# Retention and a mixture of experts on one core: a branch placed ahead of the last three scatters, the last product in two column halves, and five earlier places in the queues

## The chip, the core and the metric

The kernel runs on one core of a Trainium2 chip. The core has a matrix engine (TensorE, PE in the profile), three engines for elementwise work (VectorE or DVE, ScalarE or ACT, GpSimd or POOL), SyncE (SP), which here only issues transfers, and 16 DMA engines. Each engine works through its own instructions in their order; semaphores are what one waits for another with. The metric is the time of one execution on the device in microseconds (us), lower is better.

## The reference

Two stages, the second on the output of the first. Stage one is a linear attention with decay over 4 batches, 8 heads, 768 steps and head size 64. Stage two takes its 3072 rows of 512 numbers, picks for each the best of 8 experts by cosine similarity, and sends the row through that expert alone:

```
for t in range(S):
    state = gamma * state + k[:, :, t] (outer) v[:, :, t]
    y[:, :, t] = scale * q[:, :, t] @ state
x = y as 3072 rows of 512
logits = normalize(x) @ normalize(expert_emb).T / tau
expert_idx = argmax(logits);  gate_w = softmax(logits)[expert_idx]
for e in range(8):
    h = relu(x[mask] @ w1[e])                 # 512 -> 1024
    out[mask] = gate_w[mask] * (h @ w2[e])    # 1024 -> 512
```

## The kernel before

**Stage one, to about 108 us.** The attention goes in 12 blocks of 256 steps. Rows are written to DRAM (`xd`), their logits and ranks are formed as they come, and POOL scatters a 16 word record of each row into a table in DRAM (`tbl`), sorted by expert.

**Expert 0, to about 152 us.** The row count of an expert is only known on the chip, so each expert has a fixed number of places (`CAPS`, 360 to 408). The first 280 rows of expert 0 are gathered early into `xge`; the 128 late rows (`late`) come when the table is complete: `indices` and `gather` on POOL, then transposes on PE, a copy and a difference (`rows_high` on ACT, `rows_low` on DVE, L649 and L652). `square` (L294, ACT) sums each row's squares for the gate.

**Experts 1 to 7.** Rows are gathered (L626), written to DRAM (`write_rows`, L1064 to L1068), read back in quarters of the columns (`read_quarters`, L1083), turned on DVE and copied on ACT (`x_turn`, L1094 and L1095), with a difference on DVE (`x_low`, L1101). Every float32 operand is split in a high part and a rest, so each product takes three matmuls: `first_layer` (L261, 8 blocks `ft`), `hidden` (L266 on ACT, L267 on DVE), then the second layer. The weights come in 64 pieces of 512 KB (`load_piece` on SP, L212 and L216, into four buffers `raw`), each split by a cast on ACT (L235) and a difference on DVE (L239). Where an expert's rows don't fill whole blocks of 128, the second layer (`layer2`, L1111) makes columns of rows, which DVE turns and SP moves into `og` (`out_rows`, L1123) while the next expert runs; `finish` then scales them by the gate (L1128, ACT) and `put_rows` scatters them into the output (L1135, POOL).

**The end.** The last expert has 384 rows, three blocks of 128. For each block `layer2_rows` (L1153) makes 24 matmuls of 128 rows and 512 columns into one bank, ACT scales the bank into `og`, POOL scatters it. Then all engines read a flag (`values_load`, L1340), which says whether any expert got more rows than places, and jump by it (`tc.If`, L1384) over the code for such rows, which the given inputs don't need. Where the code is jumped over, each engine runs a short list that moves the semaphores on as if it had run (also L1384; POOL's ends with one that waits until every scatter so far has landed, and then raises the counts of its own queue). SP ends the program (L1422): it waits for each of POOL's eight DMA counts in pairs, then for eight pairs of the others, then all engines meet.

The order on each engine is the program's (`manual_schedule`), so a line of Python that moves, moves an instruction on every engine that it feeds. Quoted from the end of expert 0's first part and from the loop over the experts:

```
    nc.sync.dma_start(out=tb[:, 0, 3], in_=tbl[EARLY:CAPS[0], :2 + NE])
    slots(1)
    slots(2)
...
            if e == 1 and ft == 2:
                read_quarters(2)
```

Of the kernel before, what the change touches and what calls it, by code (L numbers as in the profile page):

```python
# [11 lines left out]
F32 = mybir.dt.float32  # L12
# [3 lines left out]
I32 = mybir.dt.int32  # L16
# [8 lines left out]
P = 128  # L25
# [82 lines left out]
def retention_moe(ctx: ExitStack, tc: tile.TileContext, q, k, v, emb, tau, w1, w2, const, const16, out):  # L108
# [42 lines left out]
    ps_ = ctxw.enter_context(tc.tile_pool(name="psT", bufs=1, space=PSUM))  # L151
    ctxw.enter_context(tc.manual_schedule(engines={ET.PE, ET.DVE, ET.Activation, ET.Pool, ET.SP}))
# [869 lines left out]
    nc.sync.dma_start(out=tb[:, 0, 3], in_=tbl[EARLY:CAPS[0], :2 + NE])  # L1022
    slots(1)
    slots(2)
    load_piece()
    run(8)
    split()
    load_piece()
    run(22)
    split()  # L1030
    load_piece()
# [3 lines left out]
    for j, n in EROWS[1:]:  # L1035
        square(xge, n, j, j)
# [96 lines left out]
    def put_rows(e, j, n, og):  # L1133

        i = nc.gpsimd.indirect_dma_start(  # L1135
            out=out[:, :], out_offset=bass.IndirectOffsetOnAxis(ap=si[:n, e, j:j + 1], axis=0),
            in_=og[:n, j, :], in_offset=None, bounds_check=NT - 1, oob_is_err=False)
        for o in put:
            tc.declare_no_dep(i.ins, o.ins, reason="other rows")
        put.append(i)  # L1140

    def layer2_rows(e, j, s, hh, hl, at):
        acc = acc_()
        n = 0
        for kt in range(FT):
            c = kt % 2
            wh, wl = piece[e * 8 + 4 + kt // 2]
            if TURNED[e]:
                wh, wl = (t.rearrange("p (t c y) -> p c t y", t=4, c=2)[:, c] for t in (wh, wl))
            else:  # L1150
                wh, wl = (t[:, c * DM:(c + 1) * DM] for t in (wh, wl))
            for x, a in ((hh, wh), (hl, wh), (hh, wl)):
                nc.tensor.matmul(acc[:s, :], x[:, kt, at], a, start=(n == 0), stop=(n == 3 * FT - 1))  # L1153
                n += 1
        return acc
# [5 lines left out]
    gather(xge, P, 0, 0, 3)  # L1161
# [15 lines left out]
    square(xge, P, 0, 3)  # L1177
    gsteps = gates(0, [(n, slice(j, j + 1), tb[:n, 0, j:j + 1, 2:]) for j, n in (*EROWS, (3, P))])
# [86 lines left out]

    for e in range(1, NE):
# [7 lines left out]
        for ft in range(FT):  # L1274
# [7 lines left out]
            if not nxt and ft == 2:  # L1282
                drained = nc.gpsimd.drain()
# [3 lines left out]
            if e == 1 and ft == 2:  # L1287
                read_quarters(2)
# [22 lines left out]
        if TURNED[e]:  # L1311
            yt = mp.tile([P, NXC, KT, Q], F32, name="yt", bufs=2)
            for dt in range(KT):
                acc = layer2(e, dt, hh, hl, c, accs[dt])
                if dt < 2:
                    finish_two()
                if dt < 2:
                    squares(e + 1, dt)
                if dt < 3:
                    next_x(e + 1, dt)  # L1320
                if dt == 1:
                    next_rows(e + 2)
                y_turn(dt, acc, yt, c)
            pend = (e, yt, og, c, groups_of(e))
        else:
            for j, n in groups_of(e):
                acc = layer2_rows(e, j, n, hh, hl, slice(j * P, j * P + n))
# [7 lines left out]
                finish(e, j, n, og, acc[:n])  # L1335
    ctxw.close()

    with tc.issue_after(drained.ins):
        tc.mark_branch_hint_location("rest", engines=(ET.Pool,))
    any_over = nc.values_load(cnti[:, 2 * NE:], min_val=0, max_val=1)  # L1340
    with ExitStack() as cx:
        op = cx.enter_context(tc.tile_pool(name="op", bufs=1))
        ps = cx.enter_context(tc.tile_pool(name="pso", bufs=2, space=PSUM))

        def expert_rows(e, i):
# [18 lines left out]
            pt = ps.tile([P, KT, P], F32, name="pt")  # L1364
# [5 lines left out]
            for ft in range(FT):  # L1370
                acc = ps.tile([P, P], F32, name="acc")
# [3 lines left out]
            py = ps.tile([P, DM], F32, name="py")  # L1375
# [8 lines left out]
        with tc.If(any_over > 0, label="rest"):  # L1384
# [11 lines left out]
            for e in range(NE):  # L1396
                nblk = nc.values_load(cnti[:, NE + e:NE + e + 1], min_val=0, max_val=NOV)
                with tc.For_i(0, nblk, 1) as i:
                    expert_rows(e, i)

# [26 lines left out]
```

## Time and profile before

| | us |
|---|---|
| median of 3 runs (lowest, highest) | 396.93 (395.78, 396.97) |
| the profiled execution's own time | 396.63 |
| its span, first to last instruction | 394.9 |
| PE busy | 385.5 |
| DVE, ACT, POOL busy | 254.4, 214.6, 154.6 |
| end of the last matmul | 388.21 |

An engine's name alone (POOL) is the engine at work; a name with q (POOLq) is its sequencer, which reads instructions, waits for semaphores, jumps and hands work to the engine, and so runs somewhat ahead of it. Times are from the start of the span. PE rows overlap: a matmul's own duration is longer than the step from one start to the next. What ended an engine's idle time stands in brackets behind a row.

### The profile page before, as it was taken

How to read it: one execution, taken by the hardware profiler on the slowest of the kernel's cores; microseconds unless marked ns; L12 is line 12 of the kernel's file. 1: busy time of each engine (PE TensorE's matmuls, PEld its weight loads, DVE VectorE, ACT ScalarE, POOL GpSimd, SP SyncE). 2: the span in 40 equal slices, each digit the busy share in tenths (PEclk: the TensorE clock that was granted, in tenths of full speed). 3: DMA queues.
4: the chain of work that ended last, by engine and by line, in shares of the span. 5: the costliest groups of instructions: out<-in, count | busy, mean ns of one | idle time of the engine just before them, and what ended most of it. 6: DMA issues, size and time to landing. Idle time of an engine off the chain costs nothing.

```text
span 394.9 us, 9644 instructions
## 1 busy us (share of the span) xinstructions
PE 385.5 (98%) x3690; PEld 359.7 (91%) x3690; DVE 254.4 (64%) x534; ACT 214.6 (54%) x382; POOL 154.6 (39%) x176
## 2 busy tenths in 40 slices
PE   8999999999999999999999999999999999999993
PEld 4898888988888899999999999999899999999982
DVE  5696876979988559835763863856457656486300
ACT  4585576666866185519446644734855625463420
POOL 2866397687752515105602512510471221211130
PEclk9999999999999999999999999999999999999998
DMA  8899899897577868876869878786999657864121
GB/s 241 261 308 288 233 257 293 219 269 197 131 241 196 286 220 300 249 176 224 286 216 262 277 251 235 230 285 187 276 266 314 196 181 242 224 225 120 39 76 59
DMA packets 91012, 89.20 MB, mean 226 GB/s; under 512 B 10781, under 2 KB 69533, under 8 KB 90956
## 3 DMA queue, kind: packets, MB, share of 16 engines
q1 hardware_dynamic: 85916, 75.39, 64.3%
q0 software_dynamic: 4864, 13.03, 9.3%
q8 instruction: 31, 0.51, 0.5%
q14 instruction: 25, 0.20, 0.2%
q10 hardware_dynamic: 176, 0.07, 0.1%
HBM read 65.00 MB, written 18.79 MB: 212 GB/s over the span
## 4 chain that ended last, share of the span: by engine, by line
PE 84%; issue 7%; DVE 4%; DMA 1%; POOL 1%; ACT 1%; POOLq 1%; SPq 0%; DVEq 0%
PE b L261 11%; PE pst L1111 11%; PE py L1111 9%; PE py L464 9%; PE py L261 9%; PE pst L261 6%; PE b L396 6%; PE b L1111 4%; PE pst L431 3%; PE pst L1153 3%; PE b L365 3%; PE b L383 3%; PE pst L1193 2%; PE b L513 2%; DMA xd<-x 1%
## 5 line engine op out<-in xcount | busy, mean ns | idle before, releaser
L239 DVE TENSOR_TENSOR wlo<-raw,whi 128x1024 fp32r<-128x1024 f32 x64 | 77.6, 1217 | 17.0 <-ACT whi L235 16.0
L1135 POOL DMA_INDIRECT out_dram<-og,si x28 | 29.6, 1058 | 120.1 <-ACT og L1128 59.4
L235 ACT CAST whi<-raw 128x1024 fp32r<-128x1024 f32 x64 | 66.1, 1044 | 1.4 <-DMA raw<-in_moe_w_dram 1.2
L626 POOL DMA_INDIRECT xr<-xd,gi x24 | 29.8, 1240 | 29.6 <-ACT sq L294 15.5
L261 PE MATMUL b<-xh,whi 128*128 128x360 f32 (+5 forms) x104 | 34.3, 334 | 0.0
L261 PE MATMUL b<-xl,whi 128*128 128x360 f32 (+5 forms) x104 | 34.2, 333 | 0.0
L261 PE MATMUL b<-xh,wlo 128*128 128x360 f32 (+5 forms) x104 | 34.1, 332 | 0.0
L417 DVE TENSOR_TENSOR pm<-b,mask 128x512 f32<-128x512 f32 x48 | 29.8, 683 | 5.0 <-PE b L396 4.8
L266 ACT ACTIVATE hh<-b 128x360 fp32r<-128x360 f32 (+5 forms) x26 | 12.6, 484 | 37.4 <-PE b L261 37.4
L354 POOL TENSOR_TENSOR hh<-whi,cst 128x512 f32<-128x512 f32 x22 | 22.7, 1045 | 20.9 <-DVE pm L417 12.1
L1111 PE MATMUL pst<-hh,wlo 128*128 128x360 f32 (+4 forms) x88 | 29.5, 336 | 1.1 <-DVE wlo L239 1.1
L1094 DVE STREAM_TRANSPOSE xt<-xg 128x384 f32<-128x384 f32 (+1 forms) x28 | 15.7, 578 | 22.3 <-DMA xg<-xs 22.2
L597 POOL DMA_INDIRECT tbl<-zt,sloti x24 | 25.5, 1062 | 11.0 <-DVE sloti L588 3.5
L1111 PE MATMUL pst<-hl,whi 128*128 128x360 f32 (+4 forms) x88 | 29.4, 334 | 0.0
L1111 PE MATMUL pst<-hh,whi 128*128 128x360 f32 (+4 forms) x88 | 29.3, 333 | 0.0
L261 PE MATMUL py<-xl,whi 128*128 128x384 f32 (+5 forms) x84 | 27.8, 335 | 0.0
L261 PE MATMUL py<-xh,whi 128*128 128x384 f32 (+5 forms) x84 | 27.5, 334 | 0.0
L261 PE MATMUL py<-xh,wlo 128*128 128x384 f32 (+5 forms) x84 | 27.3, 331 | 0.0
L359 POOL TENSOR_TENSOR hl<-wlo,cst 128x512 f32<-128x512 f32 x22 | 22.9, 1054 | 7.9 <-DMA wlo<-in_k_dram 6.7
L396 PE MATMUL b<-qT,kT 64*128 64x128 f32 x384 | 24.7, 278 | 0.1
L464 PE MATMUL py<-pm,vs 128*64 128x128 f32 x384 | 24.4, 277 | 0.1
L396 PEld LDWEIGHTS b<-qT,kT 64*128 64x128 f32 x384 | 22.4, 188 | 1.4 <-ACT yT L481 0.7
(232 smaller groups left out, 1016.2 us busy)
## 6 DMA issues: line engine op xcount, KB each, us to landing
raw<-in_moe_w_dram SPq DMA_DIRECT2D x60, 512.0 KB, 4.4
whi<-in_q_dram SPq DMA_DIRECT2D x24, 256.0 KB, 3.9
xd<-x SPq DMA_DIRECT2D x48, 128.0 KB, 6.7
wlo<-in_k_dram SPq DMA_DIRECT2D x11, 512.0 KB, 5.6
xs<-xr SPq DMA_DIRECT2D x6, 768.0 KB
og<-yt SPq DMA_DIRECT2D x72, 48.0 KB, 3.0
whi<-in_v_dram SPq DMA_DIRECT2D x6, 512.0 KB
wlo<-in_v_dram SPq DMA_DIRECT2D x6, 512.0 KB
```

The costliest lines, as they stand in the source:

```text
L235: nc.scalar.copy(out=views[1], in_=views[0])
L239: nc.vector.tensor_tensor(out=views[2], in0=views[0], in1=views[1].bitcast(F32), op=ALU.subtract)
L261: nc.tensor.matmul(acc[:, :w], a, x[:, kt, cols], start=(n == 0), stop=(n == len(todo) - 1))
L354: return eng.tensor_tensor(out=qs_r[:, m % 3, :, a], in0=qin[m % 3][:, a], in1=w, op=ALU.mult)
L359: return eng.tensor_tensor(out=ks_r[:, m % 3, s, h], in0=kin[m % 3][:, h, s], in1=w[:, h], op=ALU.mult)
L396: nc.tensor.matmul(psc[a][:, j], kTs[m][a * D:(a + 1) * D, j, u].rearrange("p s c -> p (s c)"), q_cols(m, a, j, u), start=True, stop=True, ...
L417: o.append(nc.vector.tensor_tensor(out=pm, in0=psc[a], in1=w, op=ALU.mult))
L464: nc.tensor.matmul(pys[m][u][o * D:(o + 1) * D, j], lhsT, rhs, start=first, stop=True, skip_group_check=True)
L597: i = nc.gpsimd.indirect_dma_start(out=tbl[:, :], out_offset=bass.IndirectOffsetOnAxis(ap=sloti[:, n:n + 1], axis=0), in_=zt[:, n], in_off ...
L626: return nc.gpsimd.indirect_dma_start(out=xr[:n, j, :], out_offset=None, in_=xd[:rows_, :], in_offset=bass.IndirectOffsetOnAxis(ap=gi[:n, ...
L1111: nc.tensor.matmul(acc[:, :c], a[:, f], x[:, kt, :c], start=(n == 0), stop=(n == 3 * FT - 1))
L1135: i = nc.gpsimd.indirect_dma_start(out=out[:, :], out_offset=bass.IndirectOffsetOnAxis(ap=si[:n, e, j:j + 1], axis=0), in_=og[:n, j, :], i ...
```

## The change

The last expert's third block is made in two halves of 256 columns, each in a bank of its own (`layer2_rows` with `d`). Its copies and scatters, and those of the second block, are put off in a list `rest` and issued behind the `If`; they use `xge` in place of `og`, which had been free since expert 0. The halves are scattered with a view of the output as 6144 half rows, with indices `si2` = 2 x row + half (two small DVE instructions). The PSUM pool and the order by hand last to the end of the program, so the code of the `If` takes its banks from the same pool, and the early hint to POOL of the jump's target is gone. Earlier in the program: the late rows' gather no longer has two `square`s in front of it, which go behind the late rows' own; SP loads the first piece of expert 1's weights before `slots(1)` in place of after `slots(2)`, and the next two behind the late rows' gather; in expert 1, the third expert's quarters are read one block `ft` sooner and its columns are turned and copied ahead of `finish_two` and `squares`.

```
@@ end of expert 0's first layer
     nc.sync.dma_start(out=tb[:, 0, 3], in_=tbl[EARLY:CAPS[0], :2 + NE])
+    load_expert(1)
+    load_piece()
     slots(1)
     slots(2)
-    load_piece()
     run(8)
     split()
-    load_piece()
     run(22)
     split()
-    load_piece()
     run(12)
     split()
     run(DF)
-    for j, n in EROWS[1:]:
-        square(xge, n, j, j)
...
     indices(P, 0, slice(3, 4))
-    gather(xge, P, 0, 0, 3)
+    late_rows = gather(xge, P, 0, 0, 3)
+    load_piece(late_rows)
+    load_piece(late_rows)
...
     square(xge, P, 0, 3)
+    for j, n in EROWS[1:]:
+        square(xge, n, j, j)
@@ loop over the experts
-                drained = nc.gpsimd.drain()
+                nc.gpsimd.drain()
...
-            if e == 1 and ft == 2:
+            if e == 1 and ft == 1:
                 read_quarters(2)
...
                 acc = layer2(e, dt, hh, hl, c, accs[dt])
+                if dt < 3 and e == 1:
+                    next_x(e + 1, dt)
                 if dt < 2:
                     finish_two()
                 if dt < 2:
                     squares(e + 1, dt)
-                if dt < 3:
+                if dt < 3 and e > 1:
                     next_x(e + 1, dt)
...
             for j, n in groups_of(e):
-                acc = layer2_rows(e, j, n, hh, hl, slice(j * P, j * P + n))
+                at = slice(j * P, j * P + n)
+                if nxt or (j + 1) * P < c:
+                    acc = layer2_rows(e, j, n, hh, hl, at)
+                else:
+                    for h in range(2):
+                        nc.vector.tensor_scalar(out=si2[:n, h:h + 1], in0=tb[:n, e, j, 1:2], scalar1=2.0,
+                                                scalar2=float(h), op0=ALU.mult, op1=ALU.add)
+                    rest += [(j, n, 1, h, layer2_rows(e, j, n, hh, hl, at, HALVES[h])) for h in range(2)]
                 finish_two()
...
-                finish(e, j, n, og, acc[:n])
+                if nxt or j == 0:
+                    finish(e, j, n, og, acc[:n])
+                elif j == 1:
+                    rest.append((j, n, 0, None, acc))
     ctxw.close()
 
-    with tc.issue_after(drained.ins):
-        tc.mark_branch_hint_location("rest", engines=(ET.Pool,))
+
     any_over = nc.values_load(cnti[:, 2 * NE:], min_val=0, max_val=1)
...
-        with tc.If(any_over > 0, label="rest"):
+        with tc.If(any_over > 0):
...
+    for j, n, at, h, acc in rest:
+        d = slice(0, DM) if h is None else HALVES[h]
+        nc.scalar.activation(out=xge[:n, at, d], in_=acc[:n, :d.stop - d.start], func=AF.Copy,
+                             scale=gt[:n, NE - 1, j:j + 1])
+        put_rows(NE - 1, j, n, xge, at, h)
```

POOL at the end of the program, before (`out_dram` is the output, `r` a step of the gate; the rows from the memset on are the code that is jumped over):

```order
L279 TENSOR_TENSOR r_128_4944<-r_128_4944,half 128x4
L1422 BRANCH_PREFETCH_HINT
L1135 DMA out_dram<-og,si 3072x512 x6
L1340 TENSOR_LOAD cnti
L1384 COMPARE_AND_BRANCH
L1387 MEMSET none 128x16
```

POOL at the same place with the change:

```order
L279 TENSOR_TENSOR r_128_4945<-r_128_4945,half 128x4
L1135 DMA out_dram<-og,si 3072x512 x4
L1357 TENSOR_LOAD cnti
L1400 COMPARE_AND_BRANCH
L1403 MEMSET none 128x16
```

and its last rows, behind the code that is jumped over:

```order
L1400 ISA
L1400 UNCONDITIONAL_BRANCH
L1135 DMA out_dram<-xge,si 3072x512
L1135 DMA out_dram<-xge,si_2462 6144x256 x2
L1444 UNCONDITIONAL_BRANCH
L1444 ISA
```

Six scatters ahead of the jump became four ahead of it and three behind it; ACT's list changed in the same way, with one copy of 512 and two of 256 columns behind its jump.

ACT around the late rows of expert 0, before (`sq` is the square of rows, `hr` the late rows' hidden values):

```order
L266 ACTIVATE hh<-pst_2238 128x280
L294 ACTIVATE sq,ssq_80<-xge 128x512
L294 ACTIVATE sq,ssq_80<-xge 24x512
L649 CAST xh<-b_2578 128x128
L649 CAST xh<-b_2582 128x128
L649 CAST xh<-b_2408 128x128
L649 CAST xh<-py_2228 128x128
L235 CAST whi<-raw 128x1024
L294 ACTIVATE sq,ssq_80<-xge 128x512
L1195 ACTIVATE hr<-pst_2238 128x512
```

and with the change:

```order
L266 ACTIVATE hh<-pst_2238 128x280
L649 CAST xh<-b_2575 128x128
L649 CAST xh<-b_2579 128x128
L649 CAST xh<-b_2406 128x128
L649 CAST xh<-py_2228 128x128
L235 CAST whi<-raw 128x1024
L294 ACTIVATE sq,ssq_80<-xge 128x512 x2
L294 ACTIVATE sq,ssq_80<-xge 24x512
L1200 ACTIVATE hr<-pst_2238 128x512
```

Two squares (one of 128 rows, one of 24) moved from ahead of the copies of the late rows to just ahead of `hr`. The late rows' own square stood there already.

## Rows read from the trace of the kernel before

**Rows 1.** The page's first part: engines, busy us, share of the span, instructions.

```profile
PE 385.5 (98%) x3690; PEld 359.7 (91%) x3690; DVE 254.4 (64%) x534; ACT 214.6 (54%) x382; POOL 154.6 (39%) x176
```

**Rows 2.** Waits of PE after the start: for whom, us in total, times, longest.

```profile
PE pst L1111 <- DVE wlo L239: 1.1, 2, 0.6
```

**Rows 3.** Timeline of the end: start, us, engine, line, operation, idle before.

```profile
387.82 0.39 PE L1153 MATMUL pst<-wlo,hh 128*128 128x512 f32 x1
388.25 0.69 ACT L1128 ACTIVATE og<-pst,gt 128x512 f32<-128x512 f32 x1 [4.89 <-PE pst L1153]
389.21 0.97 POOL L1135 DMA_INDIRECT out_dram<-og,si  x1 [4.59 <-ACT og L1128]
```

**Rows 4.** Sequencers at the jump's line: count, ns min/median/max, first and last start.

```profile
L1384 POOLq EVENT_SEMAPHORE  x6: 17/30/43, 392.5 to 392.9; - x6
...
L1384 ACTq EVENT_SEMAPHORE  x2: 17/17/17, 391.7 to 391.8; - x2
...
L1384 ACTq COMPARE_BRANCH  x1: 50/50/50, 388.8 to 388.8; - x1
L1384 POOLq COMPARE_BRANCH  x1: 76/76/76, 389.6 to 389.6; - x1
L1384 POOLq INC_SWDGE_SEM  x1: 312/312/312, 393.0 to 393.0; - x1
```

**Rows 5.** Sequencers at the program's end, the same columns, whole and from 393.2 to 393.35.

```profile
L1422 SPq EVENT_SEMAPHORE  x14: 17/28/28, 393.3 to 394.8; - x14
...
L1422 SPq DRAIN  x3: 7/7/13, 394.0 to 394.3; - x3
...
L1422 POOLq DRAIN  x1: 546/546/546, 393.3 to 393.3; - x1
```

**Rows 6.** The last six scatters (from 350 us on): issue to landing in us.

```profile
DMA to landing us min/median/max: 2.7/2.9/3.0
```

**Rows 7.** Two stretches of 0.2 us at the end: DMA share and GB/s stand last.

```profile
390.60:390.80 0.20, 0.00 (x0) 0.00 (x0) 0.00 (x0) 0.00 (x0) 0.00 (x0) 1.00 0.58 164
...
391.20:391.40 0.20, 0.00 (x0) 0.00 (x0) 0.00 (x0) 0.00 (x0) 0.00 (x0) 1.00 0.67 266
```

**Rows 8.** Timeline of PE: 256 column pairs of expert 0, first matmul of the last block.

```profile
138.19 0.40 PE L1193 MATMUL pst<-whi,xh 128*128 128x256 f32 x2
138.43 0.40 PE L1193 MATMUL pst<-whi,xl 128*128 128x256 f32 x2
...
382.47 0.39 PE L1153 MATMUL pst<-whi,hh 128*128 128x512 f32 x1
```

**Rows 9.** Timeline of ACT: copies out of a bank, by size.

```profile
125.84 0.41 ACT L266 ACTIVATE hh<-pst 128x280 fp32r<-128x280 f32 x1
...
371.52 0.49 ACT L266 ACTIVATE hh<-b 128x384 fp32r<-128x384 f32 x1 [1.60 <-PE b L261]
...
382.67 0.69 ACT L1128 ACTIVATE og<-pst,gt 128x512 f32<-128x512 f32 x1 [4.25 <-PE pst L1153]
```

**Rows 10.** Timeline of POOL: late gather of expert 0; fourth of the last scatters.

```profile
127.68 1.56 POOL L626 DMA_INDIRECT xge<-xd,gi  x1 [0.94 <-ACT sq L294]
...
379.37 1.02 POOL L1135 DMA_INDIRECT out_dram<-og,si  x1 [0.30 <-issue]
```

**Rows 11.** Timeline of ACT: first of the squares that move; what they precede.

```profile
126.14 0.62 ACT L294 ACTIVATE sq<-xge 128x512 bf16<-128x512 f32 x1
...
140.54 0.60 ACT L1195 ACTIVATE hr<-pst 128x512 f32<-128x512 f32 x1 [1.22 <-PE pst L1193]
```

**Rows 12.** Timeline of ACT in expert 1's second layer.

```profile
177.82 1.34 ACT L1128 ACTIVATE og<-og,gt 128x512 f32<-128x512 f32 x2 [6.51 <-DMA og<-yt]
...
180.43 0.51 ACT L1095 CAST xh<-xt 128x400 fp32r<-128x400 f32 x1
```

**Rows 13.** POOL's drain inside the last expert: sequencer, ns, start.

```profile
L1283 POOLq DRAIN  x1: 7218/7218/7218, 359.8 to 359.8; - x1
```

**Rows 14.** The scatters of table records, whole program: issue to landing in us.

```profile
DMA to landing us min/median/max: 2.1/4.1/5.7
```

More of the change, by code (lines that the diff above doesn't have):

```diff
@@ L150, in retention_moe @@
     hp = ctxw.enter_context(tc.tile_pool(name="hp", bufs=1))
-    ps_ = ctxw.enter_context(tc.tile_pool(name="psT", bufs=1, space=PSUM))
-    ctxw.enter_context(tc.manual_schedule(engines={ET.PE, ET.DVE, ET.Activation, ET.Pool, ET.SP}))
+    ps_ = ctx.enter_context(tc.tile_pool(name="psT", bufs=1, space=PSUM))
+    ctx.enter_context(tc.manual_schedule(engines={ET.PE, ET.DVE, ET.Activation, ET.Pool, ET.SP}))
     def bank(tag, bufs=1):
@@ L1131, in retention_moe, with put_rows @@
     put = []
-    def put_rows(e, j, n, og):
+    HALVES = (slice(0, DM // 2), slice(DM // 2, DM))
+    si2 = cp.tile([P, 2], I32, name="si2")
+    def put_rows(e, j, n, og, at=None, h=None):
         i = nc.gpsimd.indirect_dma_start(
-            out=out[:, :], out_offset=bass.IndirectOffsetOnAxis(ap=si[:n, e, j:j + 1], axis=0),
-            in_=og[:n, j, :], in_offset=None, bounds_check=NT - 1, oob_is_err=False)
+            out=out[:, :] if h is None else out.rearrange("t (h x) -> (t h) x", h=2),
+            out_offset=bass.IndirectOffsetOnAxis(ap=si[:n, e, j:j + 1] if h is None else si2[:n, h:h + 1], axis=0),
+            in_=og[:n, j if at is None else at, slice(0, DM) if h is None else HALVES[h]], in_offset=None, bounds_check=(NT if h is None else 2 * NT) - 1, oob_is_err=False)
         for o in put:
@@ L1140, in put_rows, with layer2_rows @@
         put.append(i)
-    def layer2_rows(e, j, s, hh, hl, at):
+    def layer2_rows(e, j, s, hh, hl, at, d=slice(0, DM)):
         acc = acc_()
@@ L1152, in layer2_rows @@
             for x, a in ((hh, wh), (hl, wh), (hh, wl)):
-                nc.tensor.matmul(acc[:s, :], x[:, kt, at], a, start=(n == 0), stop=(n == 3 * FT - 1))
+                nc.tensor.matmul(acc[:s, :d.stop - d.start], x[:, kt, at], a[:, d] if d != slice(0, DM) else a, start=(n == 0), stop=(n == 3 * FT - 1))
                 n += 1
@@ L1264, in next_rows @@
             tokens(P, e, slice(0, NG))
+    rest = []
     for e in range(1, NE):
@@ L1342, in retention_moe @@
         op = cx.enter_context(tc.tile_pool(name="op", bufs=1))
-        ps = cx.enter_context(tc.tile_pool(name="pso", bufs=2, space=PSUM))
         def expert_rows(e, i):
@@ L1363, in expert_rows @@
             run_all(gates(0, [(P, slice(0, 1), mt[:, 2:2 + NE].unsqueeze(1))]))
-            pt = ps.tile([P, KT, P], F32, name="pt")
+            pt = bank("b2").rearrange("p (k t) -> p k t", k=KT)
             for kt in range(KT):
@@ L1370, in expert_rows @@
             for ft in range(FT):
-                acc = ps.tile([P, P], F32, name="acc")
+                acc = bank(f"b{ft % 2}")[:, :P]
                 for kt in range(KT):
@@ L1374, in expert_rows @@
                 nc.scalar.activation(out=hT[:, ft], in_=acc, func=AF.Relu)
-            py = ps.tile([P, DM], F32, name="py")
+            py = bank("b3")
             for kt in range(FT):
```

## The prediction

> **What bounds the kernel now.** I read the page's first part, then the waits of PE, then the end of the timeline with the sequencers' rows, because the first two leave little else. PE is busy for 385.5 of 394.9 us [rows 1]. After its start it waits for another engine only twice, 1.1 us together, for the rest of two weight pieces on DVE [rows 2]. So nothing that only moves transfers, copies or gathers can save more than those 1.1 us, unless it ends such a wait; the rest must come from what lies behind the last matmul. That stretch is long: the last matmul starts at 387.82 and lasts 0.39, so it ends at 388.21, and the span ends at 394.9. These 6.7 us are four steps: ACT copies the bank (388.25, 0.69 us), POOL issues the scatter (389.21, 0.97 us) [rows 3], something, and the end.
>
> The "something" is in the sequencers' rows. POOL's sequencer reaches its jump at 389.6, and its next instruction, on the other side, starts at 392.5 [rows 4]: 2.8 us (392.5 less 389.6 and 0.076). ACT, with nothing to wait for from a transfer, takes as long: 388.8 to 391.7 [rows 4], 2.85 us. So I read it as the price of the jump. POOL's list of six semaphores then takes to 393.0, raising its own queue's counts 0.31 us more, and SP's first wait passes at 393.3 [rows 4, 5]. The last scatter, issued at 389.21, lands after 2.7 to 3.0 us [rows 6], so at 391.9 to 392.2: more than a microsecond before POOL lets SP go. What ends the program is therefore POOL's jump and list, not the data. From 393.3 the end takes 1.6 us, of which 0.7 us are SP's twelve waits, one after the other (393.3 to its drain at 394.0 [rows 5]), some 0.055 each.
>
> **The change part by part.**
>
> *The jump ahead of three scatters.* POOL now reaches it behind the fourth scatter, issued at 379.37 [rows 10]. The sequencer read the flag when that kind of scatter was handed over, so it jumps near 379.9 at the latest and is back near 382.8; its list waits for that fourth scatter to land, 379.37 plus 2.7 to 3.0, so at 382.4 at most; with 0.5 for the list and 0.3 for the counts it is ready by 383.6, when the second block's scatter comes up (its copy starts at 382.67 and takes 0.69 [rows 9]). ACT reads its flag behind the copy that it issues near 378, so it is back near 381.9 against 382.67. Both jumps are thus covered by the last block's products, which run from 382.47 [rows 8] to 388.2; if that cover fell short by a microsecond, only the second block's scatter would be late, and the third has 3 us more. SP's and DVE's jumps were early and stay so. Taken out of the path: everything from the landing to 393.3.
>
> *The last product by halves.* Two 256 column matmuls take 0.24 us (138.43 less 138.19) [rows 8], so 0.12 each with the weight load of each; 48 are 5.66 to 5.76. The 24 of 512 columns take 5.58 (382.47 to 387.82 is 23 steps, 0.2326 each [rows 3, 8]). The last matmul's own tail is shorter (0.28 for one, as a pair lasts 0.40 with its second starting 0.12 in, against 0.39). PE ends between 388.2 and 388.4; I take 388.3, 0.1 later. The first half is done near 385.4 and its copy and scatter lie beside the second half's product. The two index instructions on DVE stand where DVE has no more work.
>
> *The last copy.* 256 columns are not in the trace. 384 take 0.49, 280 take 0.41, 512 with the gate's scale 0.69 [rows 9, 3]. Bounds 0.4 and 0.69; I take 0.45, being nearest to the 280 row: ACT ends at 388.8, and POOL starts 0.27 later as before, at 389.05 (before: 389.21).
>
> *The last scatter.* Half the bytes. The burst of the whole one is seen from 390.6 to 391.4 [rows 7], 0.8 us; half of it gone is 0.4 at most, nothing at least. I take 0.2: it lands 2.7 after its start, at 391.75. A rule bears on it. The Trainium skill (DMA: Bandwidth & Descriptors, "Anatomy of one DMA — SWDGE (gpsimd) path") says that such a transfer costs about 2.0 us whatever its size, plus its bytes at 436 GB/s. It speaks against halves, since two pay the fixed part twice; by it 128 KB less would take 0.3 off, not 0.2, and the sum below would be 0.1 lower. Here the two halves start 2.8 us apart, so the first one's fixed part is not in the second's way.
>
> *The end.* SP now waits for the landing itself, which stands in the fourth of its twelve waits, so nine pass after it, three fewer: 0.15 saved.
>
> Sum: SP is let go at 391.75 in place of 393.3 (1.55), less 0.15 of waits: **1.7 us**, a span of 393.2. With the worst ends (copy 0.69, landing 3.0, PE 0.1 later still, no waits saved) SP is let go at 392.3 to 392.4: 1.0. With the best (copy 0.4, landing 2.5) 391.4: 2.1 with the waits.
>
> *The late rows' gather.* It waited 0.94 us for ACT's squares [rows 10]; without them it starts at most that much sooner. Nothing gained: PE never waited for these rows [rows 2]. The two squares (0.62 us each, with the read of each sum about 1.5 together) go in front of `hr`, where ACT idles 1.22 us [rows 11]; they overrun that by 0.3, and what ACT does next is 0.3 late for a PE that did not wait for any of it [rows 2]. Cost: nothing; without that idle time, 1.5 us on ACT.
>
> *The pieces of expert 1.* SP issues one about 2 us sooner, the other two after the gather has landed, perhaps 2 us later. They are cast on ACT ten microseconds on. The table read that SP issues behind the first is later by that one issue, on a path that the earlier gather shortens on POOL. Nothing.
>
> *The third expert's columns and copies.* ACT stood 6.51 us for the rows of the expert before, and copied `xh` at 180.43 only after that [rows 12]; now the copies come up to 6 us sooner and the scaled rows at most 2 us later (two copies and a weight cast), in front of scatters that nobody waits for. SP reads the quarters a block earlier, and four of its row transfers follow them by 2 us. PE had no wait at expert 2 [rows 2], so again nothing: it buys slack.
>
> The profiled execution took 396.63, 0.3 below the median of 396.93; from the median, 1.7 less is 395.2.
>
> **The rivals.** *The landing, not the jump.* The 2.8 us on POOL could be the scatter's landing, and the jump nearly free. The Trainium skill (Advanced Engine Details and Errata, "Control Flow Timing") gives a compare and branch about 0.1 us, by which no jump would be worth hiding. Then the data land at 392.5, 3.3 after issue, and with the change at 392.35: 0.95 and 0.15 of waits saved, 1.1 in all, 395.8: no change that can be told. For it: the two times lie within 0.5 us. Against it: ACT's equal 2.85 us without a transfer, and the landing row.
>
> *POOL's drain at the end.* At the end POOL drains before all engines meet. That took 0.55 us at 393.3 [rows 5], three microseconds after its last scatter; now it comes straight behind one. The other drain in the program, inside the last expert, took 7.2 us [rows 13]. If it were that again, from 389.1 to 396.3, the meeting would come 2.4 us later than before (the drain ended at 393.85): 399.3, slower. It decides from 4.8 us on. For it: nothing in the rows says what the 7.2 us were. Against it: the only drain at the end is short.
>
> *More than the end.* The 1.1 us of DVE waits go too: 394.1. Against it: DVE's order up to there is the same, and the squares that leave ACT stood behind the last of the casts that DVE needs.
>
> *A slow landing.* Table scatters took 4.1 us in the median and 5.7 at most [rows 14], on busy transfers. At 4.1 SP would go at 393.15, a gain of 0.3: 396.6. At the end nothing else moves, so I give it little.
>
> **How the numbers follow.** A measurement of this kernel can tell 0.3%, 1.2 us, from no change. Chances: forecast 0.78, landing 0.08, slow landing 0.03, drain 0.07, more than the end 0.04. The forecast alone reaches from 394.8 to 395.9 (2.1 and 1.0 less); its worst ends lie within 1.2 us, so about 0.12 of its 0.78 count as no change. Faster: 0.66 and 0.04, 0.70. The same: 0.12, 0.08 and 0.03, 0.23. Slower: 0.07. For the range I add the scatter of a median (the three runs lie 1.2 us apart): 394.4 to 396.3, which leaves out the drain, the slow landing and most of the last gain.
>
> **What would show it.** Right: POOL's and ACT's jumps near 379, the second block's scatter at 383.6 to 384, a copy of some 0.45 us, the last scatter starting near 389.0 and SP let go some 2.7 us after it; PE's DVE wait still 1.1 us; PE's end within 0.2 us of 388.2. Wrong: SP let go more than 3.5 us after the last scatter's start, a drain on POOL that ends after SP's waits, or a PE stall of half a microsecond or more anywhere between 120 and 200 us.

## The result, and the profile after

The change made the kernel slower by 0.8%: 399.96 us in the median of 12 runs against 397.01 of 12 runs of the kernel before on the same chip, a ratio of 1.0079 with an interval of 1.0061 to 1.0096. The forecast was 395.2, faster by 1.7 us. The profiled execution took 399.18, with a span of 397.3.

PE's own work is not the loss: 0.4 us more than in [rows 1], for 24 more matmuls. The page's first part of the changed kernel:

```profile
PE 385.9 (97%) x3714; PEld 360.2 (91%) x3714; DVE 254.0 (64%) x536; ACT 214.5 (54%) x383; POOL 155.5 (39%) x177
```

Its waits of PE, with the columns of [rows 2]:

```profile
PE pst L1108 <- DVE wlo L239: 1.1, 2, 0.6
PE py L784 <- DVE hl L359: 1.0, 1, 1.0
PE b L261 <- DVE wlo L239: 0.7, 1, 0.7
```

The first row is that of before. The other two are new. The one at L784 is in the first 10 us, which the change doesn't touch; 0.5 us are lost there. The last one is at the start of expert 3 and stands for more than its 0.7 us, since the matmuls ahead of it are held up too. DVE's first turn of expert 3's columns, PE's first product of expert 3 and the last of its first block, in the kernel before:

```profile
213.29 1.10 DVE L1094 STREAM_TRANSPOSE xt<-xg 128x416 f32<-128x416 f32 x2 [6.06 <-DMA xg<-xs]
...
223.47 0.34 PE L261 MATMUL b<-xh,whi 128*128 128x392 f32 x1
...
225.44 0.34 PE L261 MATMUL b<-xh,wlo 128*128 128x392 f32 x1
```

and with the change:

```profile
217.80 1.11 DVE L1091 STREAM_TRANSPOSE xt<-xg 128x416 f32<-128x416 f32 x2 [10.11 <-DMA xg<-xs]
...
223.93 0.34 PE L261 MATMUL b<-xh,whi 128*128 128x392 f32 x1
...
227.75 0.45 PE L261 MATMUL b<-xh,wlo 128*128 128x392 f32 x1 [0.69 <-DVE wlo L239]
```

From the first of these products to the last it is 2.0 us before and 3.8 with the change, and PE is 1.95 us later behind them. With the 0.5 from the first 10 us that is nearly all of the 2.5 us by which PE ends later (390.72 in place of 388.21). The columns of expert 3 came late from DMA: DVE's first turn starts 6.1 us ahead of the first product in place of 10.2. That distance is called the *lead* of an expert below. The runs of this kernel lie 6 us apart (397.64 to 403.57), and one trace doesn't say how often this happens; a second one (e5) loses 1.4 us in the same place and 0.6 at expert 2. Two kernels whose expert 0 was that of before (e4, e10) lose 0.9 us there, so expert 0's changes are not needed for it.

The end, in place of [rows 3]. Timeline of the changed kernel:

```profile
390.44 0.28 PE L1154 MATMUL py<-wlo,hh 128*128 128x256 f32 x1
...
390.76 0.47 ACT L1419 ACTIVATE xge<-py,gt 128x256 f32<-128x256 f32 x1 [2.36 <-PE py L1154]
...
387.50 1.00 POOL L1135 DMA_INDIRECT out_dram<-xge,si  x1 [4.71 <-issue]
388.80 0.97 POOL L1135 DMA_INDIRECT out_dram<-xge,si  x1 [0.30 <-issue]
391.51 0.97 POOL L1135 DMA_INDIRECT out_dram<-xge,si  x1 [1.73 <-ACT xge L1419]
```

The short copy takes 0.47, and the last scatter starts 0.79 us after PE's end (390.72), 1.0 before. But the span still ends 6.6 us after PE's end (6.7 before). The sequencers of the changed kernel at the jump (L1400) and at the end (L1444), in place of [rows 4, 5]:

```profile
L1400 POOLq EVENT_SEMAPHORE  x6: 17/30/43, 384.6 to 385.2; - x6
...
L1400 POOLq COMPARE_BRANCH  x1: 62/62/62, 381.5 to 381.5; - x1
...
L1400 PEldq COMPARE_BRANCH  x1: 3478/3478/3478, 389.0 to 389.0; - x1
...
L1444 SPq EVENT_SEMAPHORE  x14: 17/28/3673, 385.5 to 397.3; - x14
...
L1444 POOLq DRAIN  x3: 52/113/4928, 391.3 to 397.0; - x3
L1444 SPq DRAIN  x3: 7/7/13, 396.4 to 396.7; - x3
```

POOL's jump is out of the way, as forecast: 381.5 to 384.6. In its place SP waits 3.7 us for the last scatter to land, until 395.9 (4.4 us after its start), and POOL's drain lasts until 396.2. The row to look at is PE's jump. PE's sequencer runs ahead of PE; before, it reached the jump at 384.5, 4.7 us ahead of the last scatter's start, now 2.5 us ahead:

```profile
L1384 PEldq COMPARE_BRANCH  x1: 4022/4022/4022, 384.5 to 384.5; - x1
```

(That row is the kernel before.) I read it so: the matmuls that wait in PE's queue are half as long now, so the same depth of queue is half the time. Behind the jump PE reads its next code in transfers of 16 KB, the queue q8 (kind "instruction"), and the second of them meets the data of the last scatter (q0). The changed kernel's DMA queues from 393.0 to 393.6 and from 394.6 to 395.5 (packets, MB, share of 16 engines):

```profile
q0 software_dynamic: 45, 0.12, 56.0%
q8 instruction: 1, 0.02, 15.4%
...
q0 software_dynamic: 3, 0.01, 5.2%
```

Two stretches of it, with DMA share and GB/s last:

```profile
393.60:394.60 1.00, 0.00 (x0) 0.00 (x0) 0.00 (x0) 0.00 (x0) 0.00 (x0) 1.00 0.00 0
394.60:395.40 0.80, 0.00 (x0) 0.00 (x0) 0.00 (x0) 0.00 (x0) 0.00 (x0) 0.54 0.06 10
```

The one q8 packet took 1.48 us (15.4% of 16 x 0.6). 45 of the scatter's 48 packets are through by 393.6, then for a microsecond no packet starts while the code is still under way (until 394.7), and three land behind the code, the last at 395.4. Before, PE's code came from 389.2 to 390.6 and the data after it.

### The profile page after: what moved, and what is told of

The parts are those of the page before. It is cut to its first block, busy times and chain, and to the rows that moved or that the text cites. A ratio compares the mean times of both kernels' runs of the same rounds, so it can differ in the third digit from the quotient of the medians.

```text
span 397.3 us, 9699 instructions
## 1 busy us (share of the span) xinstructions
PE 385.9 (97%) x3714; PEld 360.2 (91%) x3714; DVE 254.0 (64%) x536; ACT 214.5 (54%) x383; POOL 155.5 (39%) x177
## 4 chain that ended last, share of the span: by engine, by line
PE 68%; DMA 16%; DVE 5%; SPq 3%; issue 3%; POOL 1%; ACT 1%; POOLq 0%; DVEq 0%; ACTq 0%
DMA out_dram<-og,si 10%; PE py L464 8%; PE b L261 8%; PE py L261 8%; PE pst L1108 7%; PE py L1108 6%; PE b L396 5%; PE pst L261 5%; PE b L1108 3%; PE pst L1154 3%; PE pst L431 3%; PE b L365 3%; PE b L383 2%; DMA xg<-xs 2%; SPq L1120 2%
## 5 line engine op out<-in xcount | busy, mean ns | idle before, releaser
L1135 POOL DMA_INDIRECT out_dram<-og,si x26 | 27.0, 1038 | 123.1 <-DMA xg<-xs 62.1
L626 POOL DMA_INDIRECT xr<-xd,gi x24 | 28.9, 1202 | 30.5 <-ACT sq L294 15.7
L597 POOL DMA_INDIRECT tbl<-zt,sloti x24 | 24.7, 1030 | 11.1 <-issue 3.6
L1092 ACT CAST xh<-xt 128x384 fp32r<-128x384 f32 (+4 forms) x28 | 14.3, 511 | 24.0 <-DVE xt L1091 23.7
```

The lines of the kernel that those rows point to most:

```text
L597: i = nc.gpsimd.indirect_dma_start(out=tbl[:, :], out_offset=bass.IndirectOffsetOnAxis(ap=sloti[:, n:n + 1], axis=0), in_=zt[:, n], in_off ...
L626: return nc.gpsimd.indirect_dma_start(out=xr[:n, j, :], out_offset=None, in_=xd[:rows_, :], in_offset=bass.IndirectOffsetOnAxis(ap=gi[:n, ...
L1135: i = nc.gpsimd.indirect_dma_start(out=out[:, :] if h is None else out.rearrange("t (h x) -> (t h) x", h=2), out_offset=bass.IndirectOffse ...
```

## The experiments

"End" is from the start of the last copy to the end of the span, in the profiled run; "share" is q1's share of 16 DMA engines in the first 110 us, in which every kernel moves the same 40,444 packets; "xl" is what PE waited, as expert 1 began, for the columns `xl`. The kernel before has 6.65, 80.2% and no such wait. Its own median went from 397.0 to 399.5 us with the chip, so ratios are to be compared, within their intervals.

| run | what | ratio (95%) | end | share | xl |
|---|---|---|---|---|---|
| | the change | 1.0079 (1.0061 to 1.0096) | 6.56 | 84.4 | |
| e5 | the change again | 1.0080 (1.0053 to 1.0108) | 6.35 | 83.2 | 0.5 |
| e1 | the end alone | 0.9998 (0.9979 to 1.0016) | 6.32 | 83.0 | |
| e2 | experts 0 and 1 alone | 1.0023 (1.0003 to 1.0043) | 6.39 | 80.1 | |
| e3 | the end, last block whole | 1.0032 (1.0008 to 1.0057) | 5.10 | 83.4 | |
| e4 | the halves alone | 1.0020 (1.0002 to 1.0038) | 6.90 | 83.6 | |
| e6, e12 | e1 and 8 spare matmuls | 0.9985 (0.9969 to 1.0001), 1.0002 (0.9978 to 1.0026) | 4.56, 4.56 | 84.1, 84.1 | |
| e7 | expert 0 alone | 1.0035 (1.0015 to 1.0055) | 6.63 | 80.0 | 0.8 |
| e8 | expert 1 alone | 0.9999 (0.9985 to 1.0012) | 6.47 | 80.2 | |
| e9 | the change, tables first | 1.0056 (1.0030 to 1.0081) | 4.55 | 84.5 | 0.7 |
| e10 | e6 and expert 1 | 1.0020 (0.9990 to 1.0049) | 4.56 | 84.1 | |
| e11 | the change and 8 spare matmuls | 1.0079 (1.0066 to 1.0092) | 4.55 | 84.9 | 0.7 |
| e13 | the change, tile of 64 bytes | 1.0037 (1.0011 to 1.0062) | 4.56 | 83.1 | 0.7 |
| e14 | before, and the tile of 8 bytes | 1.0052 (1.0035 to 1.0070) | 6.65 | 82.4 | |
| e15 | e6, tile of 64 bytes | 0.9955 (0.9939 to 0.9970) | 4.55 | 83.1 | |
| e16 | e15 and expert 1 | 0.9974 (0.9959 to 0.9990) | 4.56 | 83.2 | |
| e17 | e14, tile of 256 bytes | 1.0009 (0.9997 to 1.0021) | 6.71 | 80.1 | |
| e18 | e6, tile of 256 bytes | 0.9974 (0.9958 to 0.9990) | 4.56 | 80.6 | |

### The end: jump, code or drain

The whole diff of the end on an unchanged middle (e1); the middle's diff on the old end (e2); of the end's diff only the new place of the branch (e3), or only the halves (e4):

```
@@ e3, against e1: the third block whole, its scatter behind the branch too
-                if nxt or (j + 1) * P < c:
-                    acc = layer2_rows(e, j, n, hh, hl, at)
-                else:
...
+                acc = layer2_rows(e, j, n, hh, hl, at)
...
-                elif j == 1:
-                    rest.append((j, n, 0, None, acc))
+                else:
+                    rest.append((j, n, j - 1, None, acc))
@@ e4, against the kernel before, beside the halves: all scatters ahead of the branch
+    for j, n, at, h, acc in rest:
...
+        put_rows(NE - 1, j, n, xge, at, h)
     ctxw.close()
```

> The change at the end alone (branch ahead, halves), everything earlier as before. Three theories of the end. Jump (the prediction): POOL's jump was the price of the end, and the change loses its gain in the middle alone: 1.7 us faster than before, ratio 0.9957. Fetch: PE reads the code behind its jump in 16 KB transfers, which with halves run at the same time as the last scatter's data and hold it up by 1.9 us: a last landing some 3.9 us after the last scatter's start, ratio within 0.9985 and 1.002. Drain: POOL's drain at the end ends 4.7 us after the last scatter's start whatever else lands, so the span ends 5.7 us after that start, as in both kernels so far: ratio 0.9985 to 1.0. PE's end within 0.3 us of before's for all three.

> The changes of the middle alone (experts 0 and 1), the end as before. Middle theory: expert 2's gathers come some 2 us later, expert 3's some 3.7 us, and PE waits near 225 us for expert 3's columns, 1.5 to 2 us in all: ratio 1.004 to 1.007. Rival, that the shift of the profile is start-up scatter and the time is lost at the end: ratio 0.999 to 1.0015 and no such wait of PE.

> The branch ahead of the last two scatters, but the third block whole: 24 matmuls of 512 columns, one copy, one scatter of whole rows. Jump: 1.1 us faster (landing in place of POOL's list), ratio 0.997. Fetch: PE reaches its jump 3.7 us before its end as before, the 16 KB transfers end before the last scatter's data, SP is let go some 3.2 us after the last scatter's start: 1.0 us faster, ratio 0.9975. Drain: the data land as early as that, but POOL's drain ends 4.7 us after the last scatter's start and the span 5.7 us after it: no gain, ratio 0.9995 to 1.0005.

> The halves alone, with the branch behind all scatters as before. Jump: POOL jumps after its last scatter as before, which starts 0.2 us sooner: ratio 0.9995. Fetch: PE jumps late because of the halves, not because of the branch's place, so its 16 KB transfer holds up the last scatter here too, POOL's list waits for that landing: 0.3 to 0.9 us slower, ratio 1.0008 to 1.0023. Drain: it has ended when POOL comes back from its jump as before, so the last scatter's earlier start is all that shows: ratio 0.9990 to 1.0.

e1's ratio is not the jump's 0.9957, and its end of 6.32 us shows why: the last data still hold it up. e3's trace tells the other two apart. Its PE jumps 4.7 us ahead of the last scatter, as before, and the code is read before the data come. Timeline of e3, its last scatter:

```profile
391.37 0.97 POOL L1138 DMA_INDIRECT out_dram<-xge,si  x1 [2.95 <-ACT xge L1410]
```

Its queues from 391.0 to 392.8, ahead of the data, where only PE's code moves:

```profile
q8 instruction: 1, 0.02, 4.8%
```

Its sequencers at the end of the program:

```profile
L1435 POOLq DRAIN  x3: 52/113/3200, 391.1 to 395.2; - x3
L1435 SPq DRAIN  x3: 7/7/13, 394.6 to 394.9; - x3
```

The first drain ends at 394.3, 3.0 us after the last scatter's start in place of 4.7: it has no length of its own, it ends with the landing. So the drain theory fell, and the branch alone shortens the end by 1.55 us (6.65 to 5.10). In e4 the second code transfer came 0.5 us later than in e1, and the last data landed 3.0 us after the scatter's start in place of 3.65, half a microsecond before POOL was back from its jump, so they cost nothing there; its end is long because POOL jumps behind its last scatter again. e2's trace had no wait near 227 us, so that was not the middle's mark. But the times didn't follow the ends: e3 was slower than before with an end 1.55 us shorter.

### PE's jump moved out of the way, and the middle in two

```
@@ e6 and e12, against e1; e11 the same against the change; e10 with expert 1's part besides
+                    late_jump = acc_()
+                    for _ in range(8):
+                        nc.tensor.matmul(late_jump[:n, :DM // 2], hh[:, 0, at], piece[e * 8 + 4][0][:, :DM // 2], start=True, stop=True)
```

> The changed kernel once more, as it is. If its 0.8% is the kernel's own: ratio 1.006 to 1.010, and PE waits 1 to 2 us near 227 us again for expert 3's columns. Rival, that the two parts add up as they were measured apart (0.9998 and 1.0023) and the wait near 227 us comes and goes with the landings of an execution: ratio 1.000 to 1.004, with or without that wait.

> The change at the end alone, with 8 more matmuls of 256 columns behind the last half, into a bank that nobody reads. They put PE's jump some 0.96 us later and nothing else. Fetch: the second 16 KB transfer of PE's code then comes after the last scatter's data in place of among them: last data 2.4 us after the last scatter's start in place of 3.6, SP let go 1.3 to 1.9 us sooner than with the change at the end alone, span end 4.8 to 5.2 us after the last useful product (6.4 before). Against the kernel before a ratio of 0.996 to 0.997. Rival, that the landing of half rows is slow by itself or that POOL's drain has a length of its own: the end stays 6.4 us behind the last useful product, ratio 0.999 to 1.002.

> Expert 0's changes alone (pieces of expert 1 sooner, late gather ahead of the squares). Middle theory: the reads of the table stand behind a piece that waits for its buffer, so expert 1's gathers come 0.8 us later against PE and its rows and quarters 1.2 us later, but PE has slack there: ratio 1.000 to 1.002, and no wait of PE that was not there. Rival, that this part alone makes expert 3 late: ratio 1.003 to 1.006, with a wait of PE near 227 us.

> Expert 1's changes alone (third expert's quarters one block sooner, its columns and copies ahead of the scaled rows). Middle theory: SP waits for those quarters' rows in front of four to eight row transfers, so expert 1's rows are scaled 1 to 2 us later and expert 3's gathers behind them too, which PE bears unless other landings are late as well: ratio 0.999 to 1.002. Rival, that this part alone makes expert 3 late: ratio 1.003 to 1.006, with a wait of PE near 227 us.

The loss is the kernel's own (e5). Eight matmuls more, and the end is 2.1 us shorter than before, in every one of the seven traces that have them (4.55 or 4.56). e15 stands for them all. Timeline of e15, its last scatter:

```profile
392.14 0.97 POOL L1138 DMA_INDIRECT out_dram<-xge,si  x1 [1.47 <-ACT xge L1419]
```

Its sequencers, PE's jump and the end:

```profile
L1400 PEldq COMPARE_BRANCH  x1: 3538/3538/3538, 390.8 to 390.8; - x1
...
L1444 SPq EVENT_SEMAPHORE  x14: 17/28/2429, 386.1 to 395.9; - x14
L1444 POOLq DRAIN  x3: 52/113/2922, 391.9 to 395.7; - x3
```

Its queues from 393.5 to 394.3, and from 394.3 to 396.3:

```profile
q0 software_dynamic: 48, 0.13, 44.4%
...
q8 instruction: 1, 0.02, 3.3%
```

All 48 packets are through by 394.3, then comes the code. SP goes on at 394.5, 2.4 us after the scatter's start, and the drain ends at 394.8. Without the spare matmuls it is a matter of luck: in the profiled runs of the change, of e1 and of e5 the code hit the data, in those of e9 and e13, whose first transfer took 0.4 to 0.6 us longer, it came behind them and the end was 4.55 too. The Trainium skill (Runtime: NRT & Kernel Launch, "Instruction fetch mechanics") says that a taken branch out of the current pages waits for a DMA of 16 KiB blocks; the traces agree, with 16 KB packets and 3.4 to 4.3 us for PE's jump.

But e6 gained 0.15%, with an interval that holds 0, where the end of its trace is 2.1 us (0.5%) shorter.

> The changed kernel, with SP reading the two tables of experts 1 and 2 ahead of the first piece of expert 1's weights again, as before the change. If the piece in front of the tables is the loss of the middle: expert 1's first gather starts 5.0 us after the first table read in place of 6.1, its quarters come a microsecond or more sooner, and the time falls from 1.008 of the kernel before to 1.002 or less. Rival, that the loss is elsewhere (the two pieces behind the late gather, the squares, expert 1): 1.006 to 1.010 as before this edit.

> The version that should be best: the change at the end with the 8 spare matmuls, expert 1's changes, and nothing of expert 0's. If the two keep what they measured apart: span end 4.4 to 4.8 us after the start of the last copy (6.4 to 6.6 with the old end), ratio 0.995 to 0.998. Rival, that an end that is faster in the trace is not faster over many executions: 0.999 to 1.001.

> The changed kernel with the 8 spare matmuls and nothing else. If PE's code transfers hold up the last scatter in most executions of the changed kernel: span end 4.4 to 4.8 us after the last copy's start (6.35 and 6.56 without), and 0.3 to 0.5% less than the changed kernel, so 1.003 to 1.005 of the kernel before. Rival, that they do so only in the profiled ones: 1.007 to 1.009.

> The change at the end with the 8 spare matmuls once more, for a second trace and a second interval. If the first one's ratio (0.9985, 0.9969 to 1.0001) was small because of scatter before the end: 0.995 to 0.998 now, end 4.4 to 4.8 us after the last copy's start. Rival, that this end costs something earlier in the program: 0.998 to 1.001 again, with waits of PE between 5 and 200 us that the kernel before doesn't have in the same places.

e9 puts `slots(1)` and `slots(2)` ahead of `load_piece()` again. None of these did what was hoped: the best end in e10, e11 and e12 was worth nothing in the time. So these kernels must lose something ahead of the end, in code that was not changed.

Where expert 0's part loses time is seen in e7. e7 and e8 ran on the same chip, and their first table reads started 0.1 us apart. SP around the late rows, e7 (piece, tables, two pieces, rows of expert 1 written):

```profile
129.30 0.38 SPq L212 DMA_DIRECT2D raw<-in_moe_w_dram  x1
129.88 1.60 SPq L975 DMA_DIRECT2D tb<-tbl  x2
136.77 1.32 SPq L212 DMA_DIRECT2D raw<-in_moe_w_dram  x2
139.64 4.63 SPq L1061 DMA_DIRECT2D xs<-xr  x3
144.73 0.33 SPq L1065 DMA_DIRECT2D xs<-xr  x1
```

The same place in e8 (tables, three pieces, rows):

```profile
129.13 1.61 SPq L975 DMA_DIRECT2D tb<-tbl  x2
131.00 3.17 SPq L212 DMA_DIRECT2D raw<-in_moe_w_dram  x3
139.46 1.81 SPq L1064 DMA_DIRECT2D xs<-xr  x3
141.37 0.39 SPq L1068 DMA_DIRECT2D xs<-xr  x1
```

In e7 the tables stand behind a piece that waits for a buffer (0.75 us), and two pieces of 512 KB start at 136.8, while expert 1's gathered rows are landing, where in e8 all three had started by 134.2. The last rows are written 3.4 us later, and PE waits for them. The waits of PE in e7:

```profile
PE b L261 <- DVE xl L1098: 0.8, 3, 0.3
```

This wait is in five of the seven profiled kernels with expert 0's part and in none of the thirteen without it; PE falls back by 1.2 to 2.7 us there, since the matmuls between the waits are held up too. e9 put the tables first and kept it, so the tables are not the whole of it. The two pieces and the moved squares are left; I suspect the pieces, and neither was tried alone.

### The place of the tiles

What do all kernels with the new end share ahead of it? The share column: 82.4 to 84.9% with a small tile, 80.0 to 80.2% without, for the same packets. The halves need a tile `si2` of 8 bytes a partition. It takes 32, and in the program's list of places nearly all large tiles, which had been at multiples of 256 bytes, lie 32 bytes further on. No trace shows the places.

```
@@ e14, against the kernel before
+    si2 = cp.tile([P, 2], I32, name="si2")
...
+                if not nxt and j == 2:
+                    for h in range(2):
+                        nc.vector.tensor_scalar(out=si2[:n, h:h + 1], in0=tb[:n, e, j, 1:2], scalar1=2.0,
+                                                scalar2=float(h), op0=ALU.mult, op1=ALU.add)
@@ e17 and e18 (e13, e15 and e16 the same with 16 in place of 64)
-    si2 = cp.tile([P, 2], I32, name="si2")
+    si2 = cp.tile([P, 64], I32, name="si2")
```

> The changed kernel with the tile of the half rows' indices at 64 bytes a partition in place of 8, so that every tile behind it lies 64 bytes further on than before in place of 32. Place theory: the first 110 us show a DMA share of 80% for the hardware queue again (83 to 84% in the changed kernel), and the time falls from 1.008 to 1.002 to 1.005, which leaves expert 0's loss. Rival, that the place of the tiles is of no account and the loss comes from the edits of the order alone: 83 to 84% and 1.007 to 1.009 as before this edit.

> The kernel before with the tile of 8 bytes and the two small DVE instructions that fill it at the very end; nobody reads it. Place theory: 83 to 84% in the first 110 us and 1.002 to 1.006, with PE's last product 1 to 2.5 us later. Rival, that the tile is of no account: 80% and 0.999 to 1.001.

> The change at the end alone, with the 8 spare matmuls and the tile at 64 bytes. If the end's gain was hidden by the place of the tiles: 80% in the first 110 us, span end 4.55 us after the last copy's start, ratio 0.994 to 0.997, which is faster than before. Rival, that the end costs something else earlier on: 0.998 to 1.001.

> The same with expert 1's changes, without expert 0's. If expert 1's changes are worth nothing by themselves (0.9999) or guard against late landings: 0.993 to 0.997, within 0.15% of the kernel without them. Rival: slower than that one by more.

> The kernel before with the tile and its two small DVE instructions, the tile now 256 bytes a partition, so that all large tiles lie at multiples of 256 bytes again. Place theory: 80% for the hardware queue in the first 110 us (82.4% with 8 bytes) and a ratio of 0.999 to 1.001 (1.0052 with 8 bytes). Rival, that it is not the place but the tile, its two instructions, or a larger multiple: 82 to 84% and 1.003 to 1.007.

> The change at the end alone with the 8 spare matmuls, the tile at 256 bytes a partition. Place theory: 80% in the first 110 us, end 4.55 us after the last copy's start, ratio 0.993 to 0.996 (0.9955 with the tile at 64 bytes). Rival, that the place is of no account for this kernel: 83% and 0.995 to 0.998.

The hardware queue in the first 110 us: before, then the change, then e14, then e17:

```profile
q1 hardware_dynamic: 40444, 25.55, 80.2%
```

```profile
q1 hardware_dynamic: 40444, 25.55, 84.4%
```

```profile
q1 hardware_dynamic: 40444, 25.55, 82.4%
```

```profile
q1 hardware_dynamic: 40444, 25.55, 80.1%
```

The tile alone costs 0.52% (e14, 0.35 to 0.70); the same tile with the same instructions at 256 bytes costs 0.09%, with an interval that holds 0 (e17). So the loss goes with the place, and not with the tile or its instructions, with a reserve: the two ran on different chips, on which the kernel before has 397.07 and 399.05 us. Nor is the loss in e14's trace. Its profiled execution is the fastest of its ten, and PE ends at 387.89, 0.3 us sooner than in the kernel before, where 1 to 2.5 us later was expected.

My first guess, a multiple of 64 bytes, failed in the share, which stayed at 83.1 to 83.2%, while the ratios of e13 and e15 came out as it said. So the share of the first 110 us is a sign of slower transfers and not a measure of the time that they cost. The Trainium skill (DMA: Bandwidth & Descriptors, "How a descriptor splits into AXI transactions") says that reads go in pieces of at most 256 bytes from addresses that are multiples of 256, and that a descriptor which starts elsewhere fetches bytes that it doesn't use. The rows agree in direction: 2.7 to 5.9% more time for the same packets.

What slower transfers do to PE is seen in the leads. Expert 4's, whose code no edit touches, is 10.7 to 11.9 us in the six traces with the large tiles at multiples of 256 bytes (before, e2, e7, e8, e17, e18), and 8.3 to 9.1 in the fourteen others. Expert 3's lead, and what PE loses there against the kernel before:

| kernels | lead, us | loss, us |
|---|---|---|
| before, e2, e8, e17, e18 | 9.8 to 10.8 | 0 |
| e1, e3, e6, e7, e12, e14, e15 | 8.2 to 8.9 | 0 |
| e4, e10, e16 | 7.1 to 7.7 | 0.4 to 0.95 |
| e5, e9, e11, e13 | 6.5 to 6.7 | 1.35 to 1.6 |
| the change | 6.1 | 1.95 |

There is a slack here, and only what goes beyond it costs time. The tile leaves a lead of 8.9 (e14) and expert 1's changes one of 10.2 (e8), each without loss; together they leave 7.2 and 7.7 (e10, e16), and with expert 0's changes 6.1 to 6.7. At expert 2 the changes of expert 1 do buy slack: the last columns are turned 6.1 us ahead of the first product in e8 in place of 2.7. The traces that lose most there (e6, e7, e12 and e15, 1.2 to 2.9 us) don't have them.

With the tile at another place, the end's gain shows in one kernel: e15 is faster than both kernels, 395.27 us (7 runs) against 397.07 of the kernel before on that chip, 0.45% (0.30 to 0.61), or 1.8 us of the 2.1 in the trace. e18 and e16 gained 0.26% each, where 0.4 to 0.7 and 0.3 to 0.7 were expected; their intervals overlap with e15's, so neither 256 against 64 bytes nor expert 1's part is told apart by them. e15's overlaps barely with e6's, e18's well. The end alone with the tile at 8 bytes was not run on the chip of e15, so the chip is a rival for what the move gained.

## Why the prediction was wrong

- *What bounds the end* (POOL's jump and list, not the data): right. With the data free, the span ends 3.8 us after the last scatter's start (5.7 before), and e15, which has the spare matmuls, the larger tile and none of the earlier changes, gained 1.8 us where 1.7 were forecast. "The landing, not the jump" fell: it allowed 1.1 us at most, and e3's end, without POOL's jump in it, is shorter by 1.55.
- *The last scatter*, "it lands 2.7 after its start": the step that failed at the end, and it took the whole gain of 1.7 us: the end stayed at 6.6 us. I priced its bytes and left out what else moves with the halves. "SP's and DVE's jumps were early and stay so" names every jump but PE's, and PE's went from 4.7 to 2.5 us ahead of the last scatter. Its code came among the data and the landing took 4.4: the "slow landing", to which I gave 0.03, with the reason "At the end nothing else moves". The sign that I set for it, more than 3.5 us, was there.
- *The two index instructions*, "where DVE has no more work": right for the instructions, wrong for the tile they write, which was priced at nothing. By e14 it costs 0.52%, some 2 us; by the traces it takes 1.3 us or more from expert 3's lead. The order of the instructions, on which the whole sum rested, doesn't show a place in memory.
- *PE's end*, "between 388.2 and 388.4": the step that failed in the middle. It came at 390.72, and 1.95 of these 2.5 us are lost at expert 3, behind the stretch from 120 to 200 us that was named as the one to watch. [rows 2] was read as if a path on which nobody waits were free. Expert 3 had some 2 us to spare (a lead of 10.2, no loss down to 8.2), and the tile and the earlier changes together took 4.
- *The late rows' gather* and *the pieces*, "nothing": wrong, 0.35% (e7). The gather wasn't sooner: its idle time in [rows 10] was put down to ACT's squares, and without them it is the same 0.94, put down to its own indices:

```profile
128.28 1.46 POOL L626 DMA_INDIRECT xge<-xd,gi  x1 [0.94 <-POOL gi L620]
```

  So the table read was later on a path that nothing had shortened. The pieces were followed to their casts, not to the transfers that they run beside.
- *The third expert's columns*, "nothing: it buys slack": right when they are alone, 0.9999 (e8), and right that it buys slack at expert 2. With the tile it takes slack at expert 3. The scaled rows are not only "in front of scatters that nobody waits for", since expert 3's gathers stand behind those scatters on POOL.
- *POOL's drain*: not the cause. It lasted 4.9 us, but ended with the landing (e3).

The sum of what was measured apart, 0.52 for the tile, 0.35 for expert 0, 0 for expert 1 and about 0 for the end with PE's code in it, makes 0.87%, against 0.79 and 0.80 measured. That they agree is luck as far as the runs show: e1 and e2, whose two diffs make up the change, come to 0.21%. Parts that use up the same slack don't add.

Some results fit neither sum and stay open. The end alone (e1) has the tile and lost nothing; the halves alone (e4) have it too, with an end 0.25 us longer, and lost 0.20%, less than the tile by itself, though the intervals touch. The change with the spare matmuls (e11, five runs) should have gained 0.45% on the change and gained nothing. The kernels with 64 bytes (e13, e15, e16) have the shares and leads of the slow place, yet lower ratios than their like with 8. Their runs lie 3 to 9 us apart (e11's, 1 us), and a trace is one execution of each.

## What to carry to other kernels

Before a tile is added, however small, look where it pushes the tiles behind it: if DMA fills or reads them, keep them at the multiple they had, 256 bytes here. When work at the end is cut in smaller instructions, follow every sequencer that runs ahead, PE's too: what it reads behind a jump uses the same DMA engines as the last data. A wait that the trace doesn't have says there is slack, not how much: measure how far ahead of its use the data come, before and after, since edits that are free one by one can use it up together. Before queueing transfers earlier or later, see which ones they will run beside.

## What the runs showed of the hardware

- A transfer of 16 KB of PE's code, one packet, took 0.9 to 1.5 us. In the change, e1 and e5 three of a scatter's 48 packets landed only behind it, 3.7 to 3.9 us after the scatter's start; where it came after them all had landed at 2.0 (e9, e13 and those with spare matmuls).
- Tiles 32 or 64 bytes past a multiple of 256 made the same 40,444 packets keep the DMA engines busy for 82.4 to 84.9% of 110 us in place of 80.0 to 80.6%, and an expert's columns came up to 3 us later against PE (expert 4: 8.3 to 9.1 us ahead in place of 10.7 to 11.9).
- POOL's drain straight behind a scatter ended 0.6 to 0.8 us after the scatter's last packet, whenever that was (394.3 in e3, 396.2 in the change).
- Of its three scatters behind the jump, POOL started the first at 387.50, 1.7 us after the copy it needs had ended (385.77). Its sequencer issued nothing from 385.8 to 387.3, and an 8 KB transfer of code (q14) ended at 385.7; I take it for the wait for its next code.
